# Weight loads asked for from ScalarE's queue, output products 512 wide in one bank, K and Q banks read with pairs picked out, and a new order of the work in a recurrent segment

## The chip, the cores and the metric

One Trainium2 chip; the kernel runs on one of its cores. The metric is the device time of one execution in microseconds (us), the median of several runs. A core has TensorE (PE, with its weight loads shown apart as PEld), VectorE (DVE), ScalarE (ACT), GpSimd (POOL) and SyncE (SP, which here only asks for DMA transfers). Each engine works through its own list of instructions in order and waits on semaphores for the others.

## The reference

`x` has 2048 rows of 512. Two branches read it and a gate mixes them row by row:

```
g = sigmoid((x * gate_w).sum(-1));  out = g * A(x) + (1 - g) * B(x)

A: mem = mem0 (8 rows).  For each of 64 segments of 32 rows, one after the other:
     h = concat(mem, x[segment])                        # 40 rows
     q, k, v = h @ Wq, h @ Wk, h @ Wv                   # 32 heads of 128
     p = softmax(q k^T / sqrt(128), memory columns open, the rest causal)
     o = (p v) @ Wo;  mem = o[:8];  output rows o[8:]
B: 32 heads of 16, four stretches of 512 rows: causal softmax attention in a stretch,
   mixed by sigmoid(beta) with a linear memory phi(q) M / phi(q) z of the stretches before; @ wo
```

Branch A is a recurrence: the 8 memory rows of a segment are needed before the next segment's projections can start. Branch B has none that is longer than four steps.

## The kernel before, in words

**Prologue** (some 100 us). `x` is loaded in four pieces into the memory that later holds `Wo`, transposed into `xT`, and branch B's projections are made in 63 pieces (`b_projections`): keys, queries and values go through the staging tiles `stgk`, `stgq`, `stgp` and `V17` (the trace names it `V`) to memory outside the core (`scr_kTd`, `scr_qTd`, `scr_pQd`, `scr_vd`), from where they are fetched again in another layout. Between the pieces a list `weights` of 17 loads is worked off: four each of 1 MB for `Wk`, `Wq`, `Wv`, `Wo`, and `woB`. All transfers are asked for on SP, in the order in which the program is written. The tiles of the main part lie on the memory of the prologue's tiles (`late_home`); a first write there waits for the last use of what lay there. `xL`, which the first projections of the main part read, lies on `V17`.

**Main part.** `segment(s, fill)` issues one segment's units in the order that a row of `A_ORDER` gives; there are four rows, used in turn (`s % 4`). Each unit's instructions go to the engines' lists in that order. The units:

- `K0x K0y` and so on: projections (`proj`). `hT` holds the 32 rows that are the 8 memory rows and 24 rows of x. Half `b` of the heads, `x` the first and `y` the last two of four contraction steps. 16 matmuls of 512 columns for a `K0x K0y` pair, as four groups of 32 array columns side by side that write the four quarters of one bank. `k0`, `q0`, `v0` copy the bank to `KN_sb`, `QN_sb`, `V_sb`; `TK0`, `TQ0` turn K and Q by DVE's transpose of 32 by 32 blocks of pairs.
- `S` scores, `X` exponentials, `M` row sums, `L` logarithm and exponential that make the reciprocal, `N` and `n` normalise (DVE, POOL).
- `PV`, `PL`: probabilities times V, into four banks. `E0a E0b E1a E1b` copy two banks each to `OT_sb`. `PV1` takes the banks that `E0a` and `E0b` free.
- `W`: the product with `Wo` (`out_part`), four partial sums in the four quarters of the bank; `H0 H1` round the two 256-column halves to `WH`, `l0 l1` keep the remainder in `WL`, `F0 F1` (`fold`, matmuls with a 0/1 matrix) add the quarters and turn the result; `hm0 hm1` write the memory rows into the next `hT`, `ax0 ax1` the rest to `aT_st`.
- Fill: `Fc` one of the "c" units (for the 8 rows of four segments that do not fit in 32: projections `KL QL VL` from `xL`, product `ol` from `OTL`; 8 in four segments), `Ff` one of the "f" units (`of`, and the two of `tail_units`: `brow`, branch B's output product, and `atr`, which turns branch A's rows), `Fe` the copy behind it. `bS bE bP bT` are steps of branch B's attention (scores, exponential over 1024 columns, product, what follows).

A row's unit that has nothing to do leaves no instruction. `A_ENG` says which engine makes which copy. Where two engines read the same PSUM bank, `_mk_deps` makes the later reader wait for the earlier one. `evac` (L354, L356) records every copy, so that all copies share two lines; `L903` are all projections, `L959` all products with `Wo`.

Of the kernel before, what the change touches and what calls it, by code (L numbers as in the profile page):

```python
# [223 lines left out]
def build(nc, es, A_x, A_mem0, A_Wq, A_Wk, A_Wv, A_Wo, B_wq, B_wk, B_wv, B_wo, B_beta, gate_w, out, dbg=None):  # L224
    v = NS()
# [224 lines left out]
def plan_loads(v, A_x, A_mem0, A_Wq, A_Wk, A_Wv, B_wq, B_wk, B_wv, B_wo, B_beta, gate_w):  # L450
# [30 lines left out]
    for q in range(4):  # L481
        def wo(q=q):
            P.dma(grp, lambda s: s.dma_start(v.Wo_sb[:, 8 * q:8 * q + 8, :], wosrc[:, 8 * q:8 * q + 8, :]), 
                  writes=[Rs("Wo")] + ([Rs("x_sb%d" % k) for k in (2 * q, 2 * q + 1)] if q < 2 else []), name="dma_Wo%d" % q)
        pend.append(wo)
# [197 lines left out]
class BAttn:  # L683
# [159 lines left out]
    def finish(self, sb, f):  # L843
# [11 lines left out]
    bS K0x K0y Q0x Q0y K1x bP bE Q1x Q1y k0 K1y TK0 q0 bS TQ0 S0 q1 TQ1 V0x k1 bE V0y X0 TK1 V1x S1 X1 V1y M0 M1 Fc L0 bP bP Ff v0 v1 L1  # L855
    N0 N1 n0 PV0 PL0 E0a n1 Fe Ff E0b PV1 Fe PL1 W0a bT E1b W0b E1a W1b W1a bS H1 H0 Fc l0 l1 F0 hm0 F1 ax0 hm1 bE ax1 oL bT""",
    """
    bS Fe K0x K0y Q0x Q0y K1x k0 bP Q1x Q1y TK0 K1y q0 TQ0 bE S0 q1 k1 V0x bS TQ1 TK1 V0y V1x S1 X0 bE V1y X1 M0 v0 L0 M1 L1 n0 v1 Fc bP
    Ff N0 PV0 PL0 N1 E0a Fe PV1 n1 bT PL1 E0b E1a W0a E1b oL W0b W1a W1b H1 bP bS H0 Fc Ff l0 l1 F0 hm0 ax0 bE F1 hm1 Fe ax1 Ff Fe""",
    """  # L860
    bT bS K0x K0y bE k0 Q0x Q0y TK0 q0 Q1x bP K1x Q1y TQ0 q1 K1y k1 bS TQ1 bE S0 V0x V1x X0 TK1 V0y S1 v0 V1y M0 X1 L0 v1 M1 N0 L1 N1 Fc
    bP Ff Fe PV0 n0 n1 PL0 E0a PV1 bT PL1 E0b E1a W0a W0b E1b W1a W1b H1 oL H0 Fc l0 bS Ff l1 F0 hm0 F1 hm1 Fe ax1 bE ax0 bP bT""",
    """
    K0x K0y k0 Q0x TK0 Q0y q0 Q1x Q1y K1x K1y TQ0 S0 q1 V0x bS k1 TQ1 V1x TK1 V0y X0 S1 V1y M0 bE X1 M1 v0 L0 L1 Fc v1 N0 n0 PV0 PL0 Ff N1
    E0b E0a PV1 n1 bT Fe PL1 E1b Fc W0a W0b W1b E1a W1a Fe H0 bS l0 Ff H1 bP oL l1 F0 hm0 Fe bP ax0 bE bS F1 hm1 Ff ax1""")]
A_ENG = dict(E0a="dve", E0b="act", E1a="act", E1b="act", H0="dve", H1="act", K0="act", K1="act", KL0="act", KL1="act", OL="act",
             Q0="act", Q1="dve", QL0="act", QL1="act", V0="dve", V1="dve", VL0="act", VL1="act", ax="dve", hm="dve", n="gp")


def plan_a(v, nseg):  # L870
# [37 lines left out]
    def paired(nat):  # L908

        return nat.rearrange("p (m e u) -> p m u e", u=2, e=SEG)  # L910
# [6 lines left out]
    def left_units(g):  # L917
# [7 lines left out]
        for m, w_sb, wr, nat in (("K", Wk_sb, "Wk", LN_sb), ("Q", Wq_sb, "Wq", LN_sb), ("V", Wv_sb, "Wv", VL[par])):  # L925
            rn = ["LN%d" % b if m != "V" else "VL%d_%d" % (par, b) for b in range(2)]
            for b in range(2):
# [25 lines left out]
    def out_part(bks, hf, ks, first, lhs, reads, name):  # L953

        def f(pe):
            ins = None
            for k in ks:
                for j in range(4):
                    ins = pe.matmul(pb[bks[hf]][SEG * j:SEG * (j + 1), 0:HD], lhs(4 * k + j), Wo_sb[:, 4 * k + j, HD * hf:HD * (hf + 1)],  # L959
                                    start=(first and k == ks[0]), stop=False, skip_group_check=True)  # L960
            return ins
        P.op("pe", f, reads=reads + [Rs("Wo")], writes=[rbank[bks[hf]]], name="%s_%d" % (name, hf))

    def part_hi(bks, hf, hi, res, name, eng="act"):
        c = slice(HD * hf, HD * (hf + 1))
        evac(eng, hi[:, c], pb[bks[hf]][:, 0:HD], [bks[hf]], [Rs(res[0][hf])], "%sh%d" % (name, hf))

    def part_lo(bks, hf, hi, lo, res, name):
        c = slice(HD * hf, HD * (hf + 1))
        P.op("dve", lambda d: d.tensor_tensor(lo[:, c], pb[bks[hf]][:, 0:HD], hi[:, c], ALU.subtract),  # L970
             reads=[rbank[bks[hf]], Rs(res[0][hf])], writes=[Rs(res[1][hf])], name="%sl%d" % (name, hf))
        B.give(bks[hf])
# [15 lines left out]
    def ol_units(g):  # L988
# [5 lines left out]
        for b in range(2):  # L994
            def u(b=b):
                if b == 0:
                    st["bks"] = B.pair()
                for hf in range(2):
                    out_part(st["bks"], hf, range(4 * b, 4 * b + 4), b == 0, lambda h: OTL[par][:, h, :], [Rs("OTL%d" % par)], "ol%d_%d" % (g, b))
# [29 lines left out]
    def tail_units(g):  # L1029
# [11 lines left out]
        def ub():  # L1041
            bb = B.take()

            def f_(pe):
                ins = None
                for f in range(C):
                    ins = pe.matmul(pb[bb], oTg[:, f, :], woB_sb[:, f, :], start=(f == 0), stop=(f == C - 1))  # L1047
# [11 lines left out]
        def uf():  # L1059
            bk = B.take()  # L1060

            def f_atr(pe):
                ins = None
                for c in range(C):
                    ins = pe.transpose(pb16[bk][:, c * 128:(c + 1) * 128], rows[:, c, :], ident[:, :])
# [4 lines left out]
        def uf2(bk):  # L1070
            P.op("dve", lambda dv: dv.scalar_tensor_tensor(fin, pb16[bk][:, 0:512], g_sb[:, g:g + 1], t1_sb[:, :],
# [10 lines left out]
    def segment(s, fill):  # L1082
# [12 lines left out]
        def nat_ev(m, b, eng):  # L1095
# [3 lines left out]
            if m != "V":  # L1099
                dst, src = paired(dst), src.rearrange("p (m u e) -> p m u e", u=2, e=SEG)  # L1100
# [111 lines left out]
        def wo(b, half):  # L1212

            if not wb:
                wb["bks"] = B.pair()
                first = True
            else:
                first = False
# [56 lines left out]
        for b in range(2):  # L1275
# [10 lines left out]
            units["H%d" % b] = lambda b=b: part_hi(wb["bks"], b, v.WH, w_res, "wev%d" % s, ENG["H%d" % b])  # L1286
            units["l%d" % b] = lambda b=b: part_lo(wb["bks"], b, v.WH, v.WL, w_res, "wev%d" % s)
# [99 lines left out]
```

## Time and profile before

| what | value |
|---|---|
| median of 3 runs | 1009.16 us (1004.7 to 1010.88) |
| the profiled execution | 1010.23 us, of which the span shown is 1008.3 us; granted TensorE clock 0.983 |
| PE busy | 908.5 us, 90% |
| DVE, ACT, POOL busy | 62%, 62%, 25% |
| DMA | 51.65 MB; 75 to 100% of the 16 engines from 0 to 100 us, about a tenth after |
| one segment, fold to fold | 11.97 to 16.02 us, about 14 |

A segment's length is the distance between the first `fold` matmuls of neighbouring segments in the timeline. "Busy" of PE counts a matmul to its modelled end, about 0.2 us after the next one may start, so that a busy PE may still be short of work. "Idle before, <- who" names the engine whose signal ended the wait last; "issue" means that nothing the profile shows was waited for.

### The profile page before, as it was taken

How to read it: one execution, taken by the hardware profiler on the slowest of the kernel's cores; microseconds unless marked ns; L12 is line 12 of the kernel's file. 1: busy time of each engine (PE TensorE's matmuls, PEld its weight loads, DVE VectorE, ACT ScalarE, POOL GpSimd, SP SyncE). 2: the span in 40 equal slices, each digit the busy share in tenths (PEclk: the TensorE clock that was granted, in tenths of full speed). 3: DMA queues.
4: the chain of work that ended last, by engine and by line, in shares of the span. 5: the costliest groups of instructions: out<-in, count | busy, mean ns of one | idle time of the engine just before them, and what ended most of it. 6: DMA issues, size and time to landing. Idle time of an engine off the chain costs nothing. (4 is left out here: it accounts for less than half of the span.)

```text
span 1008.3 us, 56287 instructions
## 1 busy us (share of the span) xinstructions
PE 908.5 (90%) x25349; PEld 536.3 (53%) x25349; DVE 624.9 (62%) x1558; ACT 628.0 (62%) x1227; POOL 250.9 (25%) x554
## 2 busy tenths in 40 slices
PE   7997989998899999999999989999889999988896
PEld 4443555555555565555555555555555555555554
DVE  4564547565555666666677657766565776756654
ACT  4445656666666766666677657666666766656453
POOL 3611222222222222222232213222222222222110
PEclk9897999999999999999999999999999999999999
DMA  8799000010101101101011101100011111100010
GB/s 280 255 318 335 12 11 17 9 25 11 27 14 46 26 23 39 25 18 24 12 28 46 32 13 36 26 21 19 15 30 35 26 35 33 26 14 3 25 40 18
DMA packets 66007, 51.65 MB, mean 51 GB/s; under 512 B 34400, under 2 KB 64232, under 8 KB 64232
## 3 DMA queue, kind: packets, MB, share of 16 engines
q1 hardware_dynamic: 65768, 48.07, 16.3%
q8 instruction: 199, 3.26, 1.4%
q14 instruction: 40, 0.33, 0.1%
HBM read 33.47 MB, written 14.57 MB: 48 GB/s over the span
## 5 line engine op out<-in xcount | busy, mean ns | idle before, releaser
L755 ACT ACTIVATE PT<-ps 128x1024 bf16<-128x1024 f32 x160 | 161.5, 1019 | 9.3 <-PE ps L741 5.5
L354 ACT ACTIVATE KN_sb<-ps 128x512 bf16<-128x512 f32 x128 | 97.6, 762 | 87.7 <-PE ps L903 79.1
L959 PE MATMUL ps<-Wo_sb,OT_sb 128*32 128x256 bf16 x4096 | 132.2, 278 | 15.1 <-issue 13.9
L762 POOL TENSOR_SCALAR_AFFINE_SELECT PT<-PT 128x512 bf16<-128x512 bf16 (+1 forms) x96 | 75.8, 790 | 278.3 <-ACT PT L755 277.0
L903 PE MATMUL ps<-Wk_sb,hT 128*32 128x512 bf16 x2048 | 142.5, 382 | 0.3 <-DVE hT L356 0.2
L903 PE MATMUL ps<-Wv_sb,hT 128*32 128x512 bf16 x2048 | 140.9, 381 | 0.0
L903 PE MATMUL ps<-Wq_sb,hT 128*32 128x512 bf16 x2048 | 130.7, 381 | 0.0
L356 DVE CAST V_sb<-ps 128x512 bf16<-128x512 f32 x128 | 88.6, 692 | 53.0 <-PE ps L903 50.7
L959 PEld LDWEIGHTS ps<-Wo_sb,OT_sb 128*32 128x32 bf16 x4096 | 106.2, 98 | 25.5 <-issue 18.0
L354 ACT ACTIVATE OT_sb<-ps 128x320 bf16<-128x320 f32 x192 | 76.7, 435 | 53.2 <-PE ps L1196 51.4
L1173 POOL TENSOR_TENSOR P_sb<-P_sb,R_sb 128x64 bf16<-128x64 bf16 x128 | 55.5, 433 | 204.0 <-ACT R_sb L1163 164.6
L915 DVE STREAM_TRANSPOSE KT_sb<-KN_sb 128x256 f32<-128x256 f32 x128 | 56.4, 441 | 50.7 <-ACT KN_sb L354 48.1
L903 PEld LDWEIGHTS ps<-Wq_sb,hT 128*32 128x32 bf16 x2048 | 54.9, 97 | 52.6 <-issue 1.1
L1183 PE MATMUL ps<-P_sb,V_sb 32*128 32x40 bf16 x2048 | 38.0, 178 | 47.7 <-DVE OT_sb L356 31.7
L354 ACT ACTIVATE WH<-ps 128x256 bf16<-128x256 f32 x64 | 24.6, 384 | 83.7 <-PE ps L959 81.4
L903 PEld LDWEIGHTS ps<-Wk_sb,hT 128*32 128x32 bf16 x2048 | 49.0, 97 | 50.0 <-DVE hT L356 3.9
L915 DVE STREAM_TRANSPOSE QT_sb<-QN_sb 128x256 f32<-128x256 f32 x128 | 56.9, 445 | 24.9 <-ACT QN_sb L354 22.5
L354 ACT ACTIVATE LN_sb<-ps 128x512 bf16<-128x512 f32 (+1 forms) x96 | 55.3, 576 | 24.3 <-PE ps L903 12.8
L356 DVE CAST WH<-ps 128x256 bf16<-128x256 f32 x64 | 27.1, 424 | 64.7 <-PE ps L959 64.4
L1136 ACT ACTIVATE P_sb<-ps 128x224 bf16<-128x224 f32 x128 | 45.7, 357 | 34.3 <-PE ps L1127 31.9
L741 PE MATMUL ps<-QTj,KTj 32*128 32x256 bf16 (+1 forms) x768 | 64.0, 255 | 2.7 <-issue 2.5
L1183 PEld LDWEIGHTS ps<-P_sb,V_sb 32*128 32x128 bf16 x2048 | 25.5, 91 | 73.5 <-ACT OT_sb L354 52.0
(130 smaller groups left out, 1626.9 us busy)
## 6 DMA issues: line engine op xcount, KB each, us to landing
Wk_sb<-in_A_Wk_dram SPq DMA_DIRECT2D x4, 1024.0 KB, 6.8
Wq_sb<-in_A_Wq_dram SPq DMA_DIRECT2D x4, 1024.0 KB, 5.8
Wv_sb<-in_A_Wv_dram SPq DMA_DIRECT2D x4, 1024.0 KB, 7.9
Wo_sb<-in_A_Wo_dram SPq DMA_DIRECT2D x4, 1024.0 KB, 9.0
scr_vd<-V SPq DMA_DIRECT2D x16, 136.0 KB, 4.6
Vj<-scr_vd SPq DMA_DIRECT2D x32, 68.0 KB, 2.6
Wo_sb<-in_A_x_dram SPq DMA_DIRECT2D x4, 512.0 KB, 7.4
scr_kTd<-stgk SPq DMA_DIRECT2D x16, 128.0 KB, 4.5
```

Source lines behind the costliest of these rows:

```text
L354: P.op("act", lambda a: a.activation(dst, src, ACT.Copy), reads=[v.rbank[k] for k in bks], writes=dres, name=name)
L356: P.op("dve", lambda d: d.tensor_copy(dst, src), reads=[v.rbank[k] for k in bks], writes=dres, name=name)
L741: ins = pe.matmul(v.pb[bks[x]][:, 256 * e + o:256 * e + o + w], KT[e][r, 128 * kc:128 * (kc + 1)], QT[r, q0:q0 + w], start=True, stop=True ...
L755: P.op("act", lambda a: a.activation(pt[:, :, :], v.ps[:, bks[0]:bks[1] + 1, :], ACT.Exp, scale=v.SCALE_B), reads=[v.rbank[b] for b in bks ...
L762: P.op("gp", lambda g: g.affine_select(mv, mv, [[0, mv.shape[1]], [1, 128]], ALU.is_ge, 0.0, base=0, channel_multiplier=-1), reads=[rp], w ...
L903: ins = pe.matmul(pb[bk][SEG * j:SEG * (j + 1), :], lhs(c), cols(w, j) if split else w[:, 512 * j:512 * (j + 1)], start=(c == 0), stop=(c ...
L915: P.op("dve", lambda d: d.transpose(to, src), reads=reads, writes=writes, name=name)
L959: ins = pe.matmul(pb[bks[hf]][SEG * j:SEG * (j + 1), 0:HD], lhs(4 * k + j), Wo_sb[:, 4 * k + j, HD * hf:HD * (hf + 1)], start=(first and k ...
L1136: P.op("act", lambda a: a.activation(P_sb[:, b, :], pb[bk][:, 0:224], ACT.Exp, scale=SCALE), reads=[rbank[bk]], writes=[Rs("P%d" % b), Rs( ...
L1173: P.op(ENG["n"], lambda d: d.tensor_tensor(left(P_sb), left(P_sb), grp04(R_sb[:, b, :]), ALU.mult), reads=[Rs("R%d" % b)], writes=[Rs("P%d ...
L1183: ins = pe.matmul(pb[bks[j]][:, L * i:L * (i + 1)], V_sb[SEG * j:SEG * (j + 1), b, i * E:(i + 1) * E], P_sb[SEG * j:SEG * (j + 1), b, LW * ...
```

## The change

Five edits.

1. The 16 loads of 1 MB are asked for on ACT's queue, not SP's, at other places between the pieces (`n % 4 == 3 or n > 58`); the fetches of branch B's first keys and values come after all of them, and are no longer put among the pieces.
2. `out_part` writes 512 columns in one bank where it wrote 256 in each of two: half as many matmuls for `W` and `ol` (32 where there were 64, 16 where there were 32). Both halves of `H` and `l` now read one bank.
3. `paired`: the copies of K and Q read the bank with pairs picked out and write in one run; before, they read in one run and wrote every second element. The left-over K copies did it so already.
4. `brow` and `atr` run as four groups of 32 array columns, four times as many matmuls; `atr` leaves f32.
5. All four rows of `A_ORDER`, and `A_ENG`: K1, E1b, H1, QL0, VL1, OL go to DVE; Q1, H0, `hm`, `ax` to ACT.

```diff
-        if weights and (n % 5 == 0 or n > 55 and n % 2):
+        if weights and (n % 4 == 3 or n > 58):
             weights.pop(0)()
-        for at, side, part in ((30, 0, "k"), (36, 1, "k"), (40, 0, "v"), (42, 1, "v")):
-            if n == at:
-                bat.load(0, side, part)
     while weights:
         weights.pop(0)()
+    for part in "kv":
+        for G in range(2):
+            bat.load(0, G, part)
...
-              writes=[Rs(res)], name="dma_%s%d" % (res, c))
+              writes=[Rs(res)], name="dma_%s%d" % (res, c), eng="act")
...
-    K0x K0y k0 Q0x TK0 Q0y q0 Q1x Q1y K1x K1y TQ0 S0 q1 V0x bS k1 TQ1 V1x TK1 V0y X0 S1 V1y M0 bE X1 M1 v0 L0 L1 Fc v1 N0 n0 PV0 PL0 Ff N1
+    bT Q0x Q0y bP q0 K0x TQ0 K0y k0 Q1x Q1y q1 K1x K1y TK0 S0 TQ1 X0 bS V0x k1 M0 bE TK1 V0y S1 L0 V1x V1y X1 M1 L1 v0 N0 PV0 n0 PL0 n1
...
-A_ENG = dict(E0a="dve", E0b="act", E1a="act", E1b="act", H0="dve", H1="act", K0="act", K1="act", KL0="act", KL1="act", OL="act",
-             Q0="act", Q1="dve", QL0="act", QL1="act", V0="dve", V1="dve", VL0="act", VL1="act", ax="dve", hm="dve", n="gp")
+A_ENG = dict(E0a="dve", E0b="act", E1a="act", E1b="dve", H0="act", H1="dve", K0="act", K1="dve", KL0="act", KL1="act", OL="dve",
+             Q0="act", Q1="act", QL0="dve", QL1="act", V0="dve", V1="dve", VL0="act", VL1="dve", ax="act", hm="act", n="gp")
...
-    def paired(nat):
-        return nat.rearrange("p (m e u) -> p m u e", u=2, e=SEG)
+    def paired(nat, bank):
+        return nat.rearrange("p (m e u) -> p m e u", u=2, e=SEG), bank.rearrange("p (m u e) -> p m e u", u=2, e=SEG)
...
-    def out_part(bks, hf, ks, first, lhs, reads, name):
+    def out_part(bk, ks, first, lhs, reads, name):
...
-                    ins = pe.matmul(pb[bks[hf]][SEG * j:SEG * (j + 1), 0:HD], lhs(4 * k + j), Wo_sb[:, 4 * k + j, HD * hf:HD * (hf + 1)],
+                    ins = pe.matmul(pb[bk][SEG * j:SEG * (j + 1), :], lhs(4 * k + j), Wo_sb[:, 4 * k + j, :],
...
-                ins = pe.matmul(pb[bb], oTg[:, f, :], woB_sb[:, f, :], start=(f == 0), stop=(f == C - 1))
+                    for j in range(4):
+                        q = slice(SEG * j, SEG * (j + 1))
+                        ins = pe.matmul(pb[bb][q, :], oTg[:, f, q], woB_sb[:, f, :], start=(f == 0), stop=(f == C - 1))
...
-                    ins = pe.transpose(pb16[bk][:, c * 128:(c + 1) * 128], rows[:, c, :], ident[:, :])
+                    for j in range(4):
+                        q = slice(SEG * j, SEG * (j + 1))
+                        ins = pe.matmul(pb[bk][q, c * 128:(c + 1) * 128], rows[:, c, q], ident[:, :], start=True, stop=True)
```

Three places show what the order tables make of the engines' lists. The first is PE's list from the last sums of segment 24 (a segment of row 1) to its fold. Before (L1183, L1196 are `PV`, `PL`; L959 is `W`; L741 is `bS`, L788 `bP`; a projection from `xL` is an `Fc`):

```order
L903 MATMUL ps<-Wk_sb,xL 32x512 x16
L788 MATMUL ps<-PT,Vj 32x256 x8
L1183 MATMUL ps<-P_sb,V_sb 128x40 x16
L1196 MATMUL ps<-P_sb,VL 128x2x8 x16
L1183 MATMUL ps<-P_sb,V_sb 128x40 x16
L1196 MATMUL ps<-P_sb,VL 128x2x8 x16
L959 MATMUL ps<-Wo_sb,OT_sb 32x256 x64
L741 MATMUL ps<-QTj,KTj 128x256 x4
L903 MATMUL ps<-Wk_sb,xL 32x512 x16
```

After it, of the same segment (lines are a few lower or higher: L904, L1185, L1198, L957, L742, L789):

```order
L904 MATMUL ps<-Wk_sb,xL 32x512 x16
L1185 MATMUL ps<-P_sb,V_sb 128x40 x16
L1198 MATMUL ps<-P_sb,VL 128x2x8 x16
L904 MATMUL ps<-Wk_sb,xL 32x512 x16
L1185 MATMUL ps<-P_sb,V_sb 128x40 x16
L1198 MATMUL ps<-P_sb,VL 128x2x8 x16
L957 MATMUL ps<-Wo_sb,OT_sb 32x512 x32
L789 MATMUL ps<-PT,Vj 32x256 x4
L742 MATMUL ps<-QTj,KTj 128x128 x8
L789 MATMUL ps<-PT,Vj 32x256 x4
L904 MATMUL ps<-Wq_sb,xL 32x512 x16
```

An `Fc` has moved between the two `PV` (so it is in rows 1 to 3; row 4 has no `Fc` left), and `W` is half as many matmuls of twice the width; where row 1 keeps an `Fc` behind `W`, rows 3 and 4 have none there. The second place is the same segment in ACT's list, from `H` to the copies of the next segment. Before:

```order
L354 ACTIVATE WH<-ps 128x256
L755 ACTIVATE PT<-ps 128x1024
L354 ACTIVATE LN_sb<-ps 128x512
L354 ACTIVATE KN_sb<-ps 128x8x2x32
L354 ACTIVATE QN_sb<-ps 128x8x2x32
```

With the change (L756 is `bE`):

```order
L354 ACTIVATE WH<-ps 128x256
L756 ACTIVATE PT<-ps 128x1024
L354 ACTIVATE hT<-ps 128x2x8
L354 ACTIVATE aT_st<-ps 128x2x24
L354 ACTIVATE hT<-ps 128x2x8
L354 ACTIVATE aT_st<-ps 128x2x24
L756 ACTIVATE PT<-ps 128x1024
L354 ACTIVATE QN_sb<-ps 128x512
L354 ACTIVATE KN_sb<-ps 128x512
```

The four small copies `hm0 ax0 hm1 ax1` now stand in ACT's list ahead of the next segment's first copies, and Q's copy stands ahead of K's. The third place is SP's list near the end of the prologue. Before (L580 are stores of branch B, L472 and L483 the big loads):

```order
L580 DMA scr_vd<-V 128x544
L580 DMA scr_pQd<-stgp 128x512
L580 DMA scr_vd<-V 128x544 x3
L580 DMA scr_kTd<-stgk 128x512
L472 DMA Wv_sb<-in_A_Wv_dram 128x4096
L580 DMA scr_qTd<-stgq 128x512
L580 DMA scr_kTd<-stgk 128x512
L580 DMA scr_pQd<-stgp 128x512
L483 DMA Wo_sb<-in_A_Wo_dram 128x8x512
```

With the change, in ACT's list at that stage:

```order
L354 ACTIVATE stgq<-ps 128x512
L588 ACTIVATE etmp<-stgq 128x512
L484 DMA Wo_sb<-in_A_Wo_dram 128x8x512
L354 ACTIVATE V<-ps 128x32x16 x2
L484 DMA Wo_sb<-in_A_Wo_dram 128x8x512
L354 ACTIVATE stgq<-ps 128x512
L588 ACTIVATE etmp<-stgq 128x512
```

The big loads have left SP's list, and stand between ACT's copies.

More of the change, by code (lines that the diff above doesn't have):

```diff
@@ new lines @@
+    """
+    Q0x bE Q0y q0 K0x K0y k0 TQ0 Q1x Q1y TK0 bP K1x K1y S0 q1 bS X0 bE TQ1 k1 V0x M0 V0y TK1 v0 L0 S1 N0 V1x V1y X1 v1 M1 L1 Fc PV0 n0 PL0
+    N1 E0b E0a Fe Fc n1 PV1 PL1 W0a E1a E1b Fe W0b W1a bT W1b bP H0 bS oL Ff Fc bP l0 bE H1 l1 Fe Ff Fe F0 bS F1 hm0 hm1 ax1 bE ax0""",
+    """
+    Q0x bT Q0y q0 K0x K0y k0 Q1x TQ0 Q1y q1 TK0 bP K1x K1y S0 X0 bS bE TQ1 V0x M0 V0y k1 TK1 v0 S1 V1x L0 X1 N0 V1y M1 n0 Fc L1 PV0 v1 n1
+    PL0 E0b N1 E0a bT Fc PV1 PL1 W0a E1b E1a W0b Fe W1a W1b H0 l0 bP bS H1 Ff l1 bP bE Fe F0 hm0 bS F1 ax0 hm1 bE ax1 Ff Fe oL""",
@@ L1212, in wo @@
         def wo(b, half):
[L1214 to L1218, printed above, removed]
+            first = not wb
+            if first:
+                wb["bk"] = B.take()
             k = 4 * b + 2 * half
-            for hf in range(2):
-                out_part(wb["bks"], hf, (k, k + 1), first, lambda h: OT_sb[:, h, 0:SEG], [Rs("OT%d_%d" % (b, half))], "wo%d_%d%d" % (s, b, half))
+            out_part(wb["bk"], (k, k + 1), first, lambda h: OT_sb[:, h, 0:SEG], [Rs("OT%d_%d" % (b, half))], "wo%d_%d%d" % (s, b, half))
         nxt = (s + 1) % 2
```

49 lines of the change are left out of this document (21 added, 28 removed).

## The prediction

> **What bounds the kernel now.** First the page's span and engines, then two rows of the table by stages (after the stretch: PE, PEld, DVE, ACT, POOL busy, then granted clock, DMA share, GB/s).
>
> ```profile
> span 1008.3 us, 56287 instructions
> PE 908.5 (90%) x25349; PEld 536.3 (53%) x25349; DVE 624.9 (62%) x1558; ACT 628.0 (62%) x1227; POOL 250.9 (25%) x554
> ...
> q8 instruction: 199, 3.26, 1.4%
> ...
> 75.00:100.00 25.00, 16.97 (x344) 8.07 (x344) 10.80 (x24) 12.95 (x23) 2.78 (x7) 0.80 1.00 348
> ...
> 300.00:450.00 150.00, 139.31 (x4112) 83.17 (x4116) 96.50 (x249) 97.95 (x194) 36.15 (x74) 1.00 0.12 29
> ```
>
> PE is the bound: 139.31 of 150 us in mid-run, DVE and ACT at two thirds. The prologue's end is another stage: PE 16.97 of 25, DMA at 1.00, clock 0.80. So the question is where PE waits. PE's own list of waits (total, times, longest):
>
> ```profile
> PE ps L1183 <- DVE OT_sb L356: 31.7, 38, 1.0
> PE ps L959 <- issue: 14.1, 16, 1.6
> PE ps L1183 <- ACT OT_sb L354: 11.6, 14, 0.9
> PE ps L903 <- DVE etmp L590: 7.0, 1, 7.0
> PE ps L903 <- issue: 6.3, 8, 1.2
> PE ps L1183 <- DVE P_sb L1167: 3.3, 4, 0.9
> PE ps L741 <- issue: 2.5, 4, 1.3
> ```
>
> Three groups: the second `PV` waits for the copies that free its banks (31.7 + 11.6 + 3.3 = 46.6 us, 0.73 a segment); gaps with no cause shown (14.1 + 6.3 + 2.5 = 22.9 us, and smaller ones); one 7.0 us wait at the main part's start. Waits for scores, folds or `hT` hardly occur: the copies of K and Q, the exponentials and the remainder chain are hidden today.
>
> **The change, part by part.** All against the profiled run, 1010.2 us (span 1008.3 and 1.9 around it), 1 us above the median of 1009.2.
>
> *The loads.* The prologue's end, in the timeline:
>
> ```profile
> 72.43 1.57 SPq L580 DMA_DIRECT2D scr_vd<-V  x3
> 80.87 0.29 POOL L920 COPY xL<-xT 128x128 bf16<-128x128 bf16 x1 [25.38 <-DMA scr_vd<-V]
> 81.26 3.60 PE L903 MATMUL ps<-Wk_sb,xL 128*32 128x512 bf16 x32 [6.95 <-DVE etmp L590]
> 84.63 3.17 PE L903 MATMUL ps<-Wq_sb,xL 128*32 128x512 bf16 x32
> 89.15 0.47 SPq L483 DMA_DIRECT2D Wo_sb<-in_A_Wo_dram  x1
> 100.40 3.25 PE L959 MATMUL ps<-Wo_sb,OT_sb 128*32 128x256 bf16 x64
> ```
>
> `xL` lies on `V17`; its copy waited for the `scr_vd` stores, asked for at 72.43 behind big loads in SP's list and landed at 80.87. PE stood 6.95 us and came back at a low clock: 32 matmuls took 3.37 (81.26 to 84.63) and then 2.99 (3.17 less the 0.18 by which a block is modelled past its successor's start), where the rows at 503.76 and 504.62 below have 16 in 0.86, so 1.72 for 32; excess 1.65 + 1.27 = 2.9. With the loads in ACT's list the stores go out when their tiles are ready; nothing late should be left before PE's last piece. At most 9.9 us. What is late next is `Wo`: its last load was asked for at 89.15, its first use was at 100.40, and the DMA engines are full (share 1.00); if transfers end no earlier, the gain is no more than that slack. Issue is near piece 60, not behind SP's backlog, so I take **-8**, ends +3 and -10. What each load costs in ACT's own list no row shows; SP rows of the same kind last 0.47, 16 of them 7.5 us in a stage where ACT is busy 12.95 of 25: hidden, unless the queue blocks and ACT's copies come late (the end of +3).
>
> The Trainium skill ("DMA: Bandwidth & Descriptors", "Issuing engines are not separate DMA queues") says that transfers asked for by different engines share the same 16 DMA engines, and that a second issuer saves only issue time. By that the term would be near 0; the full share in the row above agrees with the first half, while the 72.43 row shows an order in one list, which a second list does remove.
>
> *The product with `Wo`.* Rows of projections and of `W`, and one gap:
>
> ```profile
> 503.76 1.04 PE L903 MATMUL ps<-Wq_sb,hT 128*32 128x512 bf16 x16
> 504.62 0.60 PE L903 MATMUL ps<-Wk_sb,hT 128*32 128x512 bf16 x8
> ...
> 512.35 1.93 PE L959 MATMUL ps<-Wo_sb,OT_sb 128*32 128x256 bf16 x64
> ...
> 432.34 1.05 PE L959 MATMUL ps<-Wo_sb,OT_sb 128*32 128x256 bf16 x31 [1.28 <-issue]
> ```
>
> 16 projection matmuls of 512 columns take 0.86 (503.76 to 504.62), 0.054 each; 64 of 256 columns take 1.75 (512.35 to the next work at 514.10, quoted below), 0.027 each. 32 of 512 take 32 x 0.054 = 1.72: streaming gains nothing. What can gain are the gaps: 14.1 us of the 22.9 fall inside `W` and `ol`, the rest on projections and branch B's scores. Instructions: `W` loses 64 x 32, `ol` 16 x 32 matmuls, 2560, each with its weight load: 5120; the tails add 16 x 24 matmuls with theirs: 768. Net 4352 of 50698, 9%, from the place where the gaps are. The row at 432.34 shows such a gap in the middle of like matmuls, with nothing waited for but the instructions themselves. I take half, **-13**, ends 0 and -23: neither end has a row for it.
>
> The Trainium skill ("Runtime: NRT & Kernel Launch", "Instruction fetch mechanics") says code comes in blocks of 16 KiB, 256 instructions, mostly hidden. The q8 row fits the first (3.26 MB in 199 packets, 16.4 KB each); if the second held, the term would be 0.
>
> *`Fc` between the two `PV`.* The wait in one segment:
>
> ```profile
> 510.79 0.28 PE L1183 MATMUL ps<-P_sb,V_sb 32*128 32x40 bf16 x16
> 511.37 0.49 DVE L356 CAST OT_sb<-ps 128x320 bf16<-128x320 f32 x1 [0.16 <-POOL P_sb L1173]
> 511.44 0.43 ACT L354 ACTIVATE OT_sb<-ps 128x320 bf16<-128x320 f32 x1
> 512.01 0.28 PE L1183 MATMUL ps<-P_sb,V_sb 32*128 32x40 bf16 x16 [0.85 <-ACT OT_sb L354]
> ```
>
> Between the `PV` 0.85 us are idle while both copies run (0.49, 0.43). An `Fc` there is 16 matmuls, 0.86: it covers the wait in rows 1 to 3 (48 segments): -46.6 x 3/4 = -35. But PV works in four row groups and `Fc` in four column groups, and a change of that kind costs: below, `Fc` to fold is 514.64 to 515.62 = 0.98 against 0.86, 0.12. Two more in 48 segments: +11.5. Net **-23**; ends 0 (the copies wait behind `N1` or another copy on DVE) and -35. Row 4 has no `Fc` left and keeps its wait.
>
> *What that `Fc` hid: `W` to fold.*
>
> ```profile
> 514.10 0.28 PE L788 MATMUL ps<-PT,Vj 128*32 128x256 bf16 x4
> 514.11 0.42 DVE L356 CAST WH<-ps 128x256 bf16<-128x256 f32 x1
> 514.39 0.38 ACT L354 ACTIVATE WH<-ps 128x256 bf16<-128x256 f32 x1 [1.11 <-PE ps L959]
> 514.57 0.76 DVE L970 TENSOR_TENSOR WL<-ps,WH 128x256 bf16<-128x256 f32 x2
> 514.64 1.05 PE L903 MATMUL ps<-Wq_sb,xL 128*32 128x512 bf16 x16
> 515.62 0.19 PE L980 MATMUL ps<-fold,WH 128*128 128x32 bf16 x1
> 515.92 0.17 DVE L356 CAST hT<-ps 128x16 bf16<-128x16 f32 x1 [0.59 <-PE ps L980]
> ```
>
> Today H0 (DVE) and H1 (ACT) run side by side from two banks; H starts 0.29 after PE is free (514.39), the second `l` ends at 515.33, and PE has bP and bS, 0.54 together (514.10 to 514.64), and `Fc` 0.98 until the fold at 515.62. Now both halves share a bank, so H0 goes first, on ACT. From PE free: 0.29 + 0.38 + hop 0.05 + l0 0.38 + hop 0.07 = 1.17 to F0; then H1 0.42 and l1 0.38: F1 at 1.97. PE's cover: row 1 bP, bS, another bP (0.22, estimated as 0.54 less 0.32 for four 256-column matmuls in two groups and their mode change), `Fc`, 1.74, and bS between F0 and F1: no wait. Row 2 the same with F0 and F1 together (about 0.15): 0.1. Row 3 bP, bS, an `of` fold (0.3, estimated from the fold's eight): 0.84, so 0.33 at F0, and 0.15 + 0.32 later 0.33 at F1. Row 4 bP, bS, bP and a 512-column step of four matmuls (0.33 by 0.21 and a mode change), 1.1: 0.07 and 0.33. Sum 1.16 in four segments, 19 us in 64; where a tail's `brow` stands at `Ff`, less. `hm` on ACT (below) adds 0.05 a segment, 3. I take **+20**, ends 0 and +30.
>
> *Copies and engines.*
>
> ```profile
> 502.06 0.60 ACT L354 ACTIVATE LN_sb<-ps 128x512 bf16<-128x512 f32 x1
> 504.04 0.77 ACT L354 ACTIVATE KN_sb<-ps 128x512 bf16<-128x512 f32 x1 [1.39 <-PE ps L903]
> 505.71 0.45 DVE L915 STREAM_TRANSPOSE QT_sb<-QN_sb 128x256 f32<-128x256 f32 x1 [0.18 <-ACT QN_sb L354]
> 516.68 1.03 ACT L755 ACTIVATE PT<-ps 128x1024 bf16<-128x1024 f32 x1
> L354 ACT ACTIVATE aT_st<-ps 128x64 bf16<-128x64 f32 x32 | 7.1, 223 | 4.6 <-PE ps L980 2.8 <-PE ps L788 0.2
> ```
>
> Run-wise writes are 0.60 on ACT (a left-over K), strided ones 0.77. PE waits for none of them, so 0 for the edit; if K0's and Q0's lay bare, -0.34 a segment, -22. On DVE no row shows that reading; by ACT's rows it lies between 0.60 and 0.77, nearer the first, and DVE is idle a third of its time: 0. `hm` and `ax`, some 0.22 each on ACT against 0.17 on DVE, now stand ahead of q0: price under the rivals.
>
> *`brow`, `atr`.*
>
> ```profile
> L1047 PE MATMUL ps<-woB_sb,oTg 128*128 128x512 bf16 x64 | 17.2, 394 | 0.0
> L1065 PE MATMUL ps<-ident,aTg 128*128 128x128 bf16 x60 | 5.8, 218 | 0.8 <-DVE WL L970 0.8
> ```
>
> Same columns in four groups, same 23 us. Beside column-group work two mode changes go, 0.12 each, at most 0.48 x 16 = 7.7; beside folds none: **-3**, ends 0 and -8.
>
> Sum: -8 - 13 - 23 + 20 - 3 = -27, 1009.2 - 27 = **982**.
>
> **Rivals.**
> *Edges give nothing:* the last transfers land when they did, so `Wo` sets the first segment, and the gaps stay. For it: the DMA share of 1.00, the small loss of instructions. Against: SP's backlog, gaps inside `W`. 982 + 8 + 13 = 1003. Chance 0.18. The two rules of the Trainium skill above would give this time.
> *Larger:* all gaps go (-10 more) and the fold chain is covered by tails (-17): 955. For it: 14.1 us of gaps sit in the very matmuls that halve. 0.20.
> *Slower, ACT's list:* after a fold ACT now has hm0, ax0, hm1, ax1 (0.9 us), often an exponential (1.03) and a left-over copy (0.60), then q0 and k0. Counted from Q0x, PE reaches the scores after four projections and a bP, 4 x 0.86 + 0.22 = 3.66. q0, k0, then TK0 (0.45, row at 505.71) need 0.6 + 0.6 + 0.1 + 0.45 = 1.75, so q0 must start by 1.9. hm1 ends near 0.45, ax1 at 0.67, the exponential at 1.7: it just fits; with a left-over copy (2.3) scores wait 0.4, and sums and PV follow late. Each 0.1 us a segment is 6.4 us; above 0.42 the change loses. At 0.8 a segment: 982 + 51 = 1033. Against: K1's copy and three others left ACT. 0.10.
> *Nothing:* the wait at PV moves behind `W` whole (-35 + 11.5 + 30) and the edges give little: 1009. 0.07.
>
> **How the numbers follow.** Forecast 982, 0.45, itself 970 to 994. Range 955 to 1004 takes in the larger and the edge case; out stay the slower one and tails. Faster by over 1% (below 999, about what a measurement can tell): 0.45 + 0.20 + a third of the edge case, 0.71; same 0.19; slower 0.10.
>
> **What would show it.** No 7 us wait before the first `Wk_sb,xL` matmul, and that matmul near 74. The second PV's wait at a third or less of 46.6, in row 4. "Issue" on the `Wo` line about half. New waits of fold on `WL`, some 20 us. If scores wait for KT or QT, the slower rival is right; if the first `W` waits for the `Wo` load, the loads term is wrong.

## The result, and the profile after

The changed kernel takes 956.2 us (median of 4 runs, 955.0 to 957.2) against 1010.0 us of the kernel before (4 runs, 1004.7 to 1016.4): ratio 0.946, 95% interval 0.941 to 0.952. The forecast was 982; the time came out where the rival "Larger" (955) had put it, 1.2 us inside the lower end of the range and 14 below the forecast's own 970 to 994. The profiled execution took 956.7 us. Its page:

```profile
span 954.7 us, 51754 instructions
PE 885.2 (93%) x23167; PEld 467.3 (49%) x23173; DVE 636.2 (67%) x1430; ACT 582.2 (61%) x1355; POOL 244.1 (26%) x554
...
q8 instruction: 182, 2.98, 1.3%
```

The same two rows of the table by stages (PE, PEld, DVE, ACT, POOL busy, granted clock, DMA share, GB/s):

```profile
75.00:100.00 25.00, 20.30 (x399) 10.22 (x404) 14.42 (x30) 11.36 (x22) 2.52 (x7) 0.86 0.80 253
300.00:450.00 150.00, 144.87 (x4020) 76.68 (x4020) 106.57 (x244) 97.93 (x228) 39.57 (x82) 1.00 0.13 30
```

PE is still the bound and now misses 5.1 of 150 us in mid-run where it missed 10.7. PE's list of waits (total, times, longest):

```profile
PE ps L979 <- DVE WL L968: 10.8, 23, 1.1
PE ps L1185 <- ACT OT_sb L354: 7.6, 11, 0.7
PE ps L1185 <- ACT R_sb L1162: 6.8, 17, 0.4
...
PE ps L1185 <- DVE OT_sb L356: 4.9, 7, 0.7
PE ps L904 <- issue: 4.8, 2, 4.3
PE ps L603 <- DVE V L356: 4.0, 2, 2.4
PE ps L979 <- DVE LN_sb L968: 3.8, 7, 2.0
...
PE ps L1122 <- DVE KT_sb L916: 1.5, 3, 0.6
```

Three things moved. The listed waits ahead of `PV` (L1185) fell from 46.6 to 19.3 us and, counted by row from the timeline, stand in row 4: there 17.2 us of these rows, in rows 1 to 3 all waits come to 0.7, 1.1 and 2.1. The two `PV` differ. Ahead of the second, all waits fell from 43.4 to 14.3 us, of which row 4 has 11.2 (8.1 before); ahead of the first, row 4 now waits 6.0 us for `R_sb` (the logarithm that reads the bank of the sums), where it had waited 2.7 for `P_sb`. The gaps called "issue" are gone but for the startup's 4.3 us and 1.6 us of short ones. The fold (L979) now waits: 10.8 on `WL`; the waits of the segments' folds are 0, 1.1, 3.3 and 6.5 in rows 1 to 4.

Where in the program was it gained? From the first fold (105.13 before, 103.10 after) to that of the last segment (999.13, 944.84) it took 894.0 us before and 841.7 after. So 52.3 us are the 63 segments between, 0.83 each, and 2 us are the start.

Some of the 52.3 is clock. The granted clock in the traces drops to 0.5 in stretches of 3.41 us. Here one follows a gap in the kernel before (rows of the timeline, then the stretch itself, with granted clock 0.50):

```profile
887.12 0.62 PE L959 MATMUL ps<-Wo_sb,OT_sb 128*32 128x256 bf16 x16 [1.28 <-issue]
...
889.48 1.90 PE L903 MATMUL ps<-Wk_sb,hT 128*32 128x512 bf16 x16
```

```profile
889.30:892.70 3.40, 3.40 (x38) 1.38 (x40) 0.73 (x3) 2.05 (x3) 2.62 (x5) 0.50 0.11 39
```

The 16 projections take 1.68 us to the next block's start, where they take 0.86 at full clock. Between the first and the last fold the kernel before has three such stretches, the changed kernel none. Half of their length is the most that they can cost PE: 5.1 us of the 52.3. The same count for the runs below is 4 in E4 (6.8 us), 5 in E7 (8.5), 8 in E9 (13.7), 11 in E8 (23.9, one of them longer) and 11 in E11 (20.5, one of them longer).

The start did not do what the loads were to do:

```profile
71.15 0.60 ACT L354 ACTIVATE V<-ps 128x512 bf16<-128x512 f32 x1 [5.52 <-DMA scr_vd<-V]
75.10 1.56 SPq L581 DMA_DIRECT2D scr_vd<-V  x3
83.27 3.60 PE L904 MATMUL ps<-Wk_sb,xL 128*32 128x512 bf16 x32 [4.28 <-issue]
99.84 1.91 PE L957 MATMUL ps<-Wo_sb,OT_sb 128*32 128x512 bf16 x32
103.10 0.19 PE L979 MATMUL ps<-fold,WH 128*128 128x32 bf16 x1
```

The stores of `V` are asked for no earlier (75.10, before 72.43), because a copy into `V` waited 5.52 us for the stores ahead of it; PE stops twice for `V` (4.0 us on L603) and again before the first `Wk_sb,xL` matmul, which comes at 83.27 where it came at 81.26. (The list calls this last wait "issue"; `xL`, which the matmul reads, was copied at 82.88 when the stores of `scr_vd` had landed.)

### The profile page after: what moved, and what is told of

Its sections match the earlier page's. It is cut to its first block, busy times and chain, and to the rows that moved or that the text cites. A ratio compares the mean times of both kernels' runs of the same rounds, so it can differ in the third digit from the quotient of the medians.

```text
span 954.7 us, 51754 instructions
## 1 busy us (share of the span) xinstructions
PE 885.2 (93%) x23167; PEld 467.3 (49%) x23173; DVE 636.2 (67%) x1430; ACT 582.2 (61%) x1355; POOL 244.1 (26%) x554
## 4 chain that ended last, share of the span: by engine, by line
PE 81%; DVE 9%; ACT 5%; DMA 2%; issue 2%; POOL 0%; ACTq 0%; DVEq 0%
PE ps L904 42%; PE ps L957 14%; PE ps L742 5%; PE ps L1185 3%; PE ps L628 2%; PE ps L979 2%; DMA scr_pQd<-stgp 2%; DVE WL L968 2%; PE ps L603 2%; PE ps L1129 2%; PE ps L1122 2%; PE ps L1155 1%; PE ps L1198 1%; PE ps L789 1%; ACT PT L756 1%
## 5 line engine op out<-in xcount | busy, mean ns | idle before, releaser
L756 ACT ACTIVATE PT<-ps 128x1024 bf16<-128x1024 f32 x160 | 163.7, 1023 | 1.5
L904 PE MATMUL ps<-Wv_sb,hT 128*32 128x512 bf16 x2048 | 141.7, 381 | 0.0
L904 PE MATMUL ps<-Wq_sb,hT 128*32 128x512 bf16 x2048 | 134.4, 380 | 0.0
L904 PE MATMUL ps<-Wk_sb,hT 128*32 128x512 bf16 x2048 | 132.7, 379 | 0.0
L957 PE MATMUL ps<-Wo_sb,OT_sb 128*32 128x512 bf16 x2048 | 123.4, 380 | 1.0 <-DVE OT_sb L356 0.4
L1175 POOL TENSOR_TENSOR P_sb<-P_sb,R_sb 128x64 bf16<-128x64 bf16 x128 | 49.1, 383 | 226.7 <-ACT R_sb L1165 114.7
L354 ACT ACTIVATE OT_sb<-ps 128x320 bf16<-128x320 f32 x128 | 56.0, 438 | 65.6 <-PE ps L1198 64.5
L354 ACT ACTIVATE QN_sb<-ps 128x512 bf16<-128x512 f32 x128 | 77.1, 603 | 30.0 <-PE ps L904 26.9
L968 DVE TENSOR_TENSOR WL<-ps,WH 128x256 bf16<-128x256 f32 x128 | 54.3, 424 | 46.6 <-ACT WH L354 42.0
L356 DVE CAST OT_sb<-ps 128x320 bf16<-128x320 f32 x128 | 62.0, 484 | 24.2 <-PE ps L1198 22.7
L904 PEld LDWEIGHTS ps<-Wk_sb,hT 128*32 128x32 bf16 x2048 | 54.0, 97 | 48.4 <-ACT KN_sb L354 0.7
L904 PEld LDWEIGHTS ps<-Wq_sb,hT 128*32 128x32 bf16 x2048 | 49.7, 96 | 44.4 <-ACT hT L354 8.5
L957 PEld LDWEIGHTS ps<-Wo_sb,OT_sb 128*32 128x32 bf16 x2048 | 48.3, 96 | 46.7 <-DVE OT_sb L356 6.8
L742 PE MATMUL ps<-QTj,KTj 32*128 32x256 bf16 (+1 forms) x768 | 62.6, 254 | 4.0 <-ACT PT L756 3.3
L1162 ACT ACTIVATE R_sb<-ps 128x160 f32<-128x160 f32 x128 | 39.1, 305 | 34.2 <-PE ps L1155 34.2
L354 ACT ACTIVATE WH<-ps 128x256 bf16<-128x256 f32 x64 | 24.6, 384 | 55.0 <-PE ps L957 51.5
L1185 PE MATMUL ps<-P_sb,V_sb 32*128 32x40 bf16 x2048 | 37.0, 178 | 21.9 <-ACT OT_sb L354 7.6
## 6 DMA issues: line engine op xcount, KB each, us to landing
Wo_sb<-in_A_Wo_dram ACTq DMA_DIRECT2D x4, 1024.0 KB, 10.1
```

What stands on the lines that cost most here:

```text
L354: P.op("act", lambda a: a.activation(dst, src, ACT.Copy), reads=[v.rbank[k] for k in bks], writes=dres, name=name)
L356: P.op("dve", lambda d: d.tensor_copy(dst, src), reads=[v.rbank[k] for k in bks], writes=dres, name=name)
L742: ins = pe.matmul(v.pb[bks[x]][:, 256 * e + o:256 * e + o + w], KT[e][r, 128 * kc:128 * (kc + 1)], QT[r, q0:q0 + w], start=True, stop=True ...
L756: P.op("act", lambda a: a.activation(pt[:, :, :], v.ps[:, bks[0]:bks[1] + 1, :], ACT.Exp, scale=v.SCALE_B), reads=[v.rbank[b] for b in bks ...
L904: ins = pe.matmul(pb[bk][SEG * j:SEG * (j + 1), :], lhs(c), cols(w, j) if split else w[:, 512 * j:512 * (j + 1)], start=(c == 0), stop=(c ...
L957: ins = pe.matmul(pb[bk][SEG * j:SEG * (j + 1), :], lhs(4 * k + j), Wo_sb[:, 4 * k + j, :], start=(first and k == ks[0]), stop=False, skip ...
```

## The experiments

Differences in us are to the changed kernel's median of 956.2; ratios are to the kernel before, timed on the same chip with each group. "Blocks start to start" are summed from the timeline between the first and the last fold.

**E1: the wide product alone.** The kernel before with `out_part` of the change (one bank, 512 columns); all else as before.

> The kernel before with one part of the change alone: the product with Wo written 512 wide into one bank; order, engines, loads, copies and tails as before. Theory (the gaps with no cause shown come from the number of PE instructions, not from where they stand): the issue waits fall from 23 us to under 6, the Wo product gets another 9 us shorter by gaps too small to be listed, the second PV still waits some 47 us, the fold waits stay under 4 because Fc still covers the chain; about 978, range 973 to 985. Rival (the gaps went because of the new order): about 1008, issue waits still near 23. The forecast's own term would put it at 997.

Measured: 1023.4 us, ratio 1.015 (1.009 to 1.022): slower than the kernel before. PE's waits:

```profile
PE ps L1183 <- DVE OT_sb L356: 31.4, 37, 1.2
PE ps L981 <- DVE WL L970: 21.6, 79, 1.1
PE ps L1183 <- ACT OT_sb L354: 11.9, 14, 0.9
PE ps L959 <- ACT R_sb L1160: 9.0, 14, 0.6
...
PE ps L788 <- issue: 1.9, 1, 1.9
PE ps L1196 <- issue: 1.1, 2, 0.6
```

The gaps went as the theory says: 3 us are left of some 25, and between the folds the blocks of `W` are another 7.8 us shorter. The time did not follow, since two waits came instead: 21.6 us of the fold for `WL`, and 9.0 us of the left-over product `ol` (L959 with `OTL`). The first is the chain that the forecast priced at 20, and the rows of one segment show it in the old order:

```profile
512.88 0.28 PE L788 MATMUL ps<-PT,Vj 128*32 128x256 bf16 x4
513.17 0.38 ACT L354 ACTIVATE WH<-ps 128x256 bf16<-128x256 f32 x1 [1.05 <-PE ps L959]
513.58 0.42 DVE L356 CAST WH<-ps 128x256 bf16<-128x256 f32 x1 [0.73 <-ACT WH L354]
...
514.52 0.19 PE L981 MATMUL ps<-fold,WH 128*128 128x32 bf16 x1
```

DVE's half starts when ACT's half of the same bank has ended, as `_mk_deps` orders them (before, both ran side by side), and the fold comes 1.64 us after PE is free, just past its cover of `bP`, `bS` and `Fc`. My theory was wrong to leave this out for the old order: the wide product by itself is no gain. The profile is of the shortest of the four runs (1013.8 us at a granted clock of 0.992; the others took 1018.4 to 1028.7 at 0.986 to 0.973). Its span is 3.5 us longer than that of the kernel before; the rest of the 13 us between the medians is in runs at a lower clock, of which no trace is kept.

**E2: the loads back on SP.** The changed kernel, with the two `eng="act"` and the places of the loads undone.

> The changed kernel with the weight loads, their places and the branch-B loads put back as before (on SP); all else as changed. Theory (the DMA engines are the limit in the prologue, so the list that asks for a load hardly matters): 2 us slower, range 0 to +4, about 958; the wait ahead of the first Wk_sb,xL matmul is about 7 us in one piece again, but the first fold comes within 2.5 us of where it is in the changed kernel. Rival (the forecast's term): 8 us slower, 964 or more.

Measured: 956.3 us, ratio 0.947 (0.944 to 0.950); difference 0.1. The wait is one piece again, and PE's start moves by 0.6:

```profile
83.86 3.60 PE L903 MATMUL ps<-Wk_sb,xL 128*32 128x512 bf16 x32 [8.53 <-DVE etmp L590]
```

The first fold comes at 105.22 instead of 103.10, as early as in the kernel before, and the last one 0.7 later than in the changed kernel. The list that asks for the weights is worth nothing at the end of the run; the rival's 8 us is out.

**E3: the same product in twice as many matmuls.** The changed kernel with

```diff
-                    ins = pe.matmul(pb[bk][SEG * j:SEG * (j + 1), :], lhs(4 * k + j), Wo_sb[:, 4 * k + j, :],
...
+                    for c in (slice(0, HD), slice(HD, 2 * HD)):
+                        ins = pe.matmul(pb[bk][SEG * j:SEG * (j + 1), c], lhs(4 * k + j), Wo_sb[:, 4 * k + j, c],
...
```

What `W` adds up here is not the reference's, probably since both halves open a sum in the one bank, which no run separates; the matmuls are as many and as wide as before.

> The changed kernel with each 512-wide matmul of the Wo product issued as two of 256 columns into the two halves of the same bank: the same columns, banks, order and copies, 2560 more matmuls and their weight loads. Theory (instruction count makes the gaps): issue waits of 12 to 25 us come back, and the time rises by 20 to 33, to 976 to 989. Rival (the order removed the gaps; count costs nothing): 956, within 4 us, issue waits under 4.

Measured: 980.8 us, ratio 0.971 (0.968 to 0.974); difference +24.6 (+20.4 between the profiles). The gaps are back, most of them in `W`:

```profile
PE ps L958 <- issue: 8.8, 13, 1.2
...
PE ps L904 <- issue: 5.7, 3, 5.0
```

5.0 of the second row is the start. The listed gaps are about half of the 20; the rest are stops too short for the list, as in the blocks of `W` (117.2 against 113.0 us, start to start, less the listed waits). With order, banks and copies held, 2560 matmuls and their weight loads cost 20 to 25 us (at most 1.7 of it clock: one stretch).

The kept traces say what the gaps are. Number PE's records in order: matmuls, weight loads, semaphore instructions. In the kernel before, all 31 gaps called "issue" between the first and the last fold end at number 193 or 194 of a stretch of 256, each of them 1.2 to 1.6 us after a packet of 16,384 bytes of the page's "q8 instruction" had landed. Measured against the usual step from one matmul to the next, these two places hold 35 us more than two places do on average, stops too short for the list included. In E1 they hold 3 us more, in E3 18, and in the changed kernel no two neighbouring places hold more than 3. So PE stood until the next block of its instructions had come. The number of these packets differs little (199 before, 179 in E1, 182 in the changed kernel, 202 in E3), which speaks for the density of instructions in `W` and against their number; no run changes one alone.

**E4: the old order with all else changed.** `A_ORDER` and `A_ENG` of before.

> The changed kernel with the unit order and the engine table of before; wide product, loads, copies and tails as changed. Theory: issue waits stay under 6 us, the second PV waits 45 us again (21 in the changed kernel), fold waits fall from 16 to under 4, the order is worth 10 to 16 us: 966 to 972. Rival (the order removed the gaps): issue waits near 20 us, 985 or more. Rival (the order is worth nothing, what it gains at PV it loses at the fold): 956, within 4.

Measured: 1026.1 us, ratio 1.017 (1.013 to 1.020); difference +70. It is E1 with a later start: 902.3 us between first and last fold (E1 899.2), and at the start `bS`, which the old row 1 has in front, waits for its load, where the new row 1 has a projection:

```profile
PE ps L742 <- DMA QTj<-scr_qTd: 3.8, 1, 3.8
```

The 10 to 16 us expected were far too low: given the wide product, the order is worth about 60 us between the folds. The rival's "985 or more" is met by the number alone, since its gaps did not come back (the one "issue" row, 4.1 us, is the start). The other way round, the new order with two banks, was not run.

**E5: the filler behind the second PV.** In rows 1 to 3 "Fc PV1 PL1" becomes "PV1 PL1 Fc".

> The changed kernel with one filler moved: the Fc that rows 1 to 3 have between the two PV stands directly behind the second PV and its left-over part. Theory (the forecast's own term: the filler covers a wait of 0.73 us in 48 segments and costs two mode changes of 0.12): second-PV waits rise from 21 to about 56 us, mode changes give 11 back, the time rises by 23, range 16 to 36, to about 979. Rival (what the copies make PE wait for there, it would wait for a little later at W anyway): within 5 of 956.

Measured: 989.5 us, ratio 0.978 (0.974 to 0.981); difference +33.3.

```profile
PE ps L1185 <- DVE OT_sb L356: 37.9, 47, 1.0
...
PE ps L1185 <- ACT OT_sb L354: 9.7, 14, 0.7
```

All waits at L1185, small ones too, rise from 21.9 to 58.3 us; rows 1 to 3 now have 13.6, 13.5 and 12.7 of them. The filler is worth 33: the wait was priced rightly, the mode changes taken off it were too dear (below).

**E6: strided copies, and E10: whole-array tails.** One with the copies of K and Q written as before, one with `brow` and `atr` as before.

> The changed kernel with the copies of K and Q of the segments written strided as before; all else as changed. Theory (the copies lie beside PE's work): the three ACT copies take 0.77 instead of 0.60, PE's waits for KT and QT grow by less than 3 us, the time is within 4 us of 956. Rival (in the new order K0's and Q0's copies lie on the path to the scores): 0.17 for each of two copies in 64 segments, 22 us slower, 978.

> The changed kernel with brow and atr over the whole array again, as before. Theory (the forecast's term of 3 us for two mode changes a piece): 959, range 956 to 964, all of it in the 16 segments that hold these pieces. Rival (no cost): 956, within 2.

Measured: 958.8 us, ratio 0.949 (0.944 to 0.953), and 957.7 us, ratio 0.946 (0.942 to 0.951). On ACT a copy of Q takes 767 ns strided and 597 by runs (medians), and ACT is busy 31 us less by it (613.7 and 582.2); the kernel gains some 3: between the folds 845.5 against 841.7 us. The tails are worth 1.2 there. Neither difference stands clear of the intervals.

**E7: the sums side by side.** In each row M0 moves to just ahead of M1, and L0, N0, n0 behind.

> The changed kernel with one unit moved in each row: the first half's sums (M0) stand directly ahead of the second half's (M1) as before, and what needs them (reciprocal, normalising) behind. Theory (part of the gain that the forecast did not have is that the new order takes the two sums apart, so that neither waits inside its own block for its exponential): the sums' blocks, start to start, grow from 16 to about 29 us and the first PV waits a little in rows 2 and 4; 10 to 20 us slower, about 970. Rival (the sums' place is worth nothing): within 4 of 956.

Measured: 1024.2 us, ratio 1.013 (1.008 to 1.018); difference +68, several times both expectations.

```profile
PE ps L1185 <- DVE P_sb L1169: 27.5, 47, 1.1
PE ps L1185 <- DVE V_sb L356: 19.3, 16, 1.6
PE ps L1122 <- DVE V_sb L356: 12.8, 16, 0.8
```

The sums' own blocks did not grow (15.8 against 16.2 us, less the waits behind them), so the mechanism in my theory is not shown. What the rows show is that `PV` and the scores (L1122) wait for DVE. The likely reason, which no run tests by itself, is that with M0, L0 and N0 late DVE has the `V` copies and both normalisings in one place.

**E8, E9: two tries at row 4's wait.** E8 moves a filler from row 1 to row 4's PV and puts the `ol` fillers first; E9 moves row 4's first `bS` there and its `bE` behind E1a.

> A version meant to be better than the changed kernel: row 4 gets a filler between its two PV, taken from row 1 (the one ahead of the first PV), with the fillers of the out rows first in each group so that the banks suffice. Theory (the second PV's wait is now row 4's alone, 17 us of 21, and row 1 waits for nothing): the row 4 waits go, two mode changes in 16 segments cost 4, row 1 loses some 0.2 us a segment at the second PV; 6 to 12 us faster than the changed kernel, about 947. Rival (row 1's filler covered the chain from the second sums to the second PV, and the left-over parts now come late): 956 to 966.

> A second version meant to be better than the changed kernel, with the fillers left where they are: in row 4 branch B's scores step that stands between the first half's exponential and its sums moves between the two PV, and its exponential behind the last output copy on ACT. Theory (row 4's second PV waits 0.7 us a time, a scores step of 0.33 works in the same row groups and needs banks that are free there): the row 4 waits fall from 17 to about 12, and the first PV's 0.4 us wait for the normalising, 6 us in all, goes too since ACT does not stand in a branch-B exponential then; 5 to 10 us faster than the changed kernel, about 949. Rival (the exponential now stands ahead of WH on ACT and the fold comes later by what PV gains; or the sums miss the cover): 954 to 965.

Measured: 1033.4 us, ratio 1.020 (1.016 to 1.025), and 982.0 us, ratio 0.970 (0.966 to 0.974). E8's first row below, E9's other two:

```profile
PE ps L979 <- DVE LN_sb L968: 32.1, 16, 2.1
```

```profile
PE ps L742 <- ACT OT_sb L354: 9.7, 14, 0.7
PE ps L957 <- DVE OT_sb L356: 7.9, 12, 0.7
```

In E8 the fold of the out rows came straight behind its products, and waited 2 us for its remainder 16 times; its stretches at half clock come to up to 23.9 us more. In E9 `bS` itself waits for the copies that PV had waited for, since its banks are theirs, and then `W` waits for the copies behind. So the wait moved and did not shrink: between the folds all waits over 0.15 us rose by 11.3 us. Up to 13.7 of E9's 25.8 us there are clock: each of its eight stretches stands just behind 3.41 us in which PE had idled 1.45 to 1.92 us (the idlest 3.41 us of the changed kernel hold 1.55, and none follows). Both runs lie outside both of their expectations. A cover must not need what the wait is for.

**E11: the old engine table.** `A_ENG` of before in the new order.

> The changed kernel in its new unit order, with the engine table of before (K1, H1, E1b, hm, ax and others back on their old engines). Theory (the order was laid out around its table; after E7 a copy behind another on DVE is what breaks it): hm and ax on DVE save the scores' inputs 0.05 a segment (3 us), but Q1's copy and the V copies now share DVE in another sequence and H0, l0, l1 stand on one engine; 10 to 40 us slower, 966 to 996, with PV and the scores waiting for DVE copies. Rival (the table is worth nothing beside the order): within 4 of 956.

Measured: 1081.8 us, ratio 1.070 (1.063 to 1.076); difference +126.

```profile
PE ps L1122 <- DVE KT_sb L916: 23.8, 49, 1.1
PE ps L742 <- ACT PT L756: 22.4, 22, 1.1
```

Scores wait for KT, `bS` for exponentials. Order and table are one thing; half of it is worse than none.

**E12: fewer bytes beside the stores.** `if len(weights) > 5 and n % 3 == 2`: the first twelve loads earlier, `Wo` behind the last piece.

> The changed kernel with other places for the weight loads on ACT: the twelve of Wk, Wq and Wv behind every third piece of the prologue instead of every fourth, the four of Wo behind the last piece. Theory (after E2: not the list but the bytes in flight hold up the stores of V; 4 MB of Wo stand beside those stores, and the DMA engines have a hole near 40 us): the stores of scr_vd asked for near 72 to 75 land in 4 to 5 us instead of 6 and more, the first Wk_sb,xL matmul comes at 77 to 80 instead of 83.3, the first W may wait up to 2 us for Wo; 2 to 5 us faster than the changed kernel, 951 to 954. Rival (the same bytes end at the same time, so what the stores gain the first W waits for Wo): 956, within 1.5.

Measured: 955.7 us (6 runs), ratio 0.946 (0.943 to 0.949).

```profile
74.99 1.91 PE L904 MATMUL ps<-Wk_sb,xL 128*32 128x512 bf16 x32
75.79 7.42 ACTq L484 DMA_DIRECT2D Wo_sb<-in_A_Wo_dram  x4
83.96 1.90 PE L904 MATMUL ps<-Wq_sb,hT 128*32 128x512 bf16 x16 [3.60 <-ACT LN_sb L354]
92.46 0.39 PE L742 MATMUL ps<-QTj,KTj 32*128 32x256 bf16 x4 [3.03 <-DMA QTj<-scr_qTd]
99.16 1.91 PE L957 MATMUL ps<-Wo_sb,OT_sb 128*32 128x512 bf16 x32
```

Here the main part does start at 75, 8 us sooner, as the forecast had wanted of the change, and the stores land in 1.9 us. Nothing comes of it: the four `Wo` loads stand on ACT for 7.42 us, ACT's first copies wait behind them, `bS` waits for its load, and the first `W` comes 0.7 us sooner. The rival's time was right, but no wait of `W` for `Wo` is listed: what gave the start back were ACT's late copies and that load.

## Why the prediction was right and wrong

*The loads, -8: wrong.* The first fold came 2 us sooner, which E2 undoes, but E2's time differs by 0.1: nothing was left of it at the end. The step that failed is "the stores go out when their tiles are ready": it took a place in SP's list for the cause, where the landing of the stores ahead was, with full DMA engines. The clause on what is late next was the better half: E12 starts PE at 75 and ends where it ended. The Trainium skill ("DMA: Bandwidth & Descriptors", "Issuing engines are not separate DMA queues") had put the term near 0; E2's 0.1 us agrees.

*Gaps in the product, -13: right place, too small.* Nearly all of them went, and E3 prices them at 20 to 25; by their places in PE's list they were 35 before, and 3 were left in E1. Taking half of the 23 us that are listed left out what is too short for the list. The Trainium skill ("Runtime: NRT & Kernel Launch", "Instruction fetch mechanics") calls the crossing of code blocks mostly hidden. In the changed kernel the trace agrees (182 packets, no more than 3 us at any two places); in the kernel before it does not (199 packets, 35 us).

*Fc between the PV, -23: right place, too small.* The -35 for the covered wait stands (36 us came back in E5), although the 46.6 it was taken from counted 3.3 us ahead of the first `PV`: rows 1 to 3 had 35.3 us ahead of the second. The 11.5 for mode changes does not: E5's 33 leaves about 3. One segment's rows show why:

```profile
322.26 0.25 PE L1198 MATMUL ps<-P_sb,VL 32*128 32x16 bf16 x16
322.44 1.05 PE L904 MATMUL ps<-Wv_sb,xL 128*32 128x512 bf16 x16
323.42 0.27 PE L1185 MATMUL ps<-P_sb,V_sb 32*128 32x40 bf16 x16
323.54 0.25 PE L1198 MATMUL ps<-P_sb,VL 32*128 32x16 bf16 x16
323.71 1.91 PE L957 MATMUL ps<-Wo_sb,OT_sb 128*32 128x512 bf16 x32
```

From column groups to row groups `Fc` takes 0.98, the 0.12 over 0.86; the step from row groups to `Fc` (0.18) is as long as that to `W` (0.17), which was there before: one change is paid, not two. (The forecast's 0.12 came from `Fc` to the fold, which is another kind of change; from `Fc` to `PV` it is as much.) Row 4 kept its wait at the second `PV`, as said, and got one at the first.

*W to fold, +20: about right, in another shape.* All waits ahead of the segments' folds rose from 2.0 to 11.8 us and those of the out rows' folds from 2.0 to 5.8, and the blocks of both grew by another 8, start to start less those waits: 14 to 22 in all. Rows 1, 2 and 4 came as worked out (0, 1.6, 6.4 expected, 0, 1.1, 6.5 measured); row 3 was priced 10.6 and waited 3.3.

*Tails, -3; copies, 0:* about 1 and 3, neither told from 0.

The sum by experiments: loads 0, gaps -25, Fc -33, tails and copies -4, fold about +14 on the listed waits: -48 of -54. No experiment assigns the remaining 6. Between the folds the traces hold three terms that the forecast had not: up to 5.1 us of half clock gone, the blocks of the sums (start to start) 10.1 shorter, those of the scores' left-over part (L1127 before, L1129 after) 5.9 longer. With the gaps at 35 and not 25 they overlap with the terms above and are not added to them.

*What the sum could not see.* The terms were priced one by one on the old order. E1, E4, E7 and E11 show that they do not stand apart: the wide product without the new order is 13 us slower than before, the order without its engine table 69 us slower (medians, each against the kernel before of its own group). The forecast had half of the gain and the right sign, not the right worth of each piece.

*Luck.* That "Larger" met the time is luck. Of its two conditions the gaps went, but the fold chain was not covered: all waits ahead of the folds, small ones too, rose from 4.0 to 17.6 us. What it lacked there, and the 8 us of the loads, was made up by gaps larger than its 23, by `Fc` and by terms that the forecast did not have. "Slower, ACT's list" did not happen: scores wait for KT and QT some 2 us in all.

## What to carry over

Half as many, wider matmuls stream no faster here, but PE's instructions come less densely, and its stops for the next block of them go, some of them too short for a list of waits. The price in this kernel is that the copies behind them read one bank, one after the other; look for the cover of that chain before counting the gain. Judge a transfer by when its bytes end: PE's 8 us earlier start in E12 was given back within 25 us. A unit covers a wait only if its own banks and queues are free of what is waited for, and an order is measured whole. Compare the granted clock of two profiles before putting a difference down to the waits alone.

## What was not expected of the hardware

- Four 1 MB loads asked for back to back kept ACT's queue for 7.42 us (E12: 0.42, 0.55, 2.72 and 3.58), where single ones 1.7 to 9.8 us apart took 0.33 to 0.41 each in the changed kernel.
- Stops of PE with no named cause fall where a new stretch of 256 of its instructions begins, at most 1.6 us after a packet of instructions landed: 35 us in the kernel before, no more than 3 at any two places in the changed one. At equal columns, 5120 instructions more brought 18 of them back (E3).
- The granted clock went to 0.5 for 3.41 us at a time: eight times between the folds of E9, each time behind 3.41 us with 1.45 to 1.92 us of idle PE, and never between the folds of the changed kernel.
